# First chunk of a gated long convolution: q's rows in 128-partition transfers, let go by steps of step two

## The chip, the cores and the metric

The kernel runs on one core of one Trainium2 chip. The metric is the device time of one launch in microseconds (us): the median of three runs before the change is 697.23 us. Times inside the run come from one profiled execution and are counted from the start of its span. PE is the matrix engine (TensorE), DVE is VectorE, ACT is ScalarE, POOL is GpSimd, SP is SyncE, which here only starts transfers.

## The reference

What is computed, cut to what matters (B = 1, S = 2048 rows, D = 640 channels, F = 1728):

```python
x = A_q
mod = (_silu(c) @ w_mod).reshape(c.shape[0], 6, 1, -1)
sa, ca, ga, sb, cb, gb = (mod[:, i] for i in range(6))
h = _layernorm(x, axis=-1) * (1 + ca) + sa
# _A_ref: a 4-tap causal filter of k, times v, a long causal
# convolution with ssm_k per channel (by FFT), plus kv * ssm_D, times h
x = x + ga * _A_ref(h, A_k, A_v, A_shift_k, A_ssm_k, A_ssm_D)
h = _layernorm(x, axis=-1) * (1 + cb) + sb
# _B_ref: layernorm, then w2 @ gelu(w1 @ .) over the 2048 rows
x = x + gb * _B_ref(h, B_w1, B_b1, B_w2, B_b2)
```

So the first gate needs three things: q's rows with their mean and variance, the first half of `silu(c) @ w_mod` (1920 of its 3840 columns), and the long convolution.

## The kernel before, in words

**Tiling.** The 640 channels go in five chunks `c` of 128. A partition holds 64 positions of two half chunks of 64 channels; q's 2048 rows lie in two tiles `xa` and `xb` (views `XH`, `XR(j)`) with row `32*i + 16*b + j` in partition `64*b + i`, column block `j` (0 to 15).

**One chunk of the convolution.** `kv_ops` multiplies k's four taps and v into `X` (four groups of 8 operations; group 2 often on POOL, the others on DVE, in part handed out between other work by `dv(n)` from the list `fill`). `step1(0, t)` transforms `X` on PE (line 230), `step1(1, t)` the filter `ssm_k`, which `load_ks` brings into `aux`, `perm_add` adds `ssm_D` to, and `perm` lays into the tile `p`. Step two is `f2(g)`, g = 0 to 7 (line 246): 64 matmuls into PSUM, one half copied out by ACT (`kt`), two products by DVE (`p`), two additions by POOL (`y`). `i2` (line 275) and `i1` (line 294) transform back, and `gate` multiplies into `A1` (the second half of `aux`) and adds to x.

**The first chunk has more in it.** While chunk 0 goes through step two, q is loaded. Its statistics (`bn_stats`, 16 column blocks, two reads and one merge each) come on DVE behind the loop, `rstd` after them. `mod_load` brings w_mod's 1920 columns in five pieces of 128 rows (983,040 bytes each), `mod_part` multiplies each on PE (line 354) as soon as its turn in PE's order comes, `mod_sum` and `mod_row` (line 365) spread the sums to all partitions, then `a1_ops` makes the normalised rows (`ac`, on ACT, from `rs1` and `nm1`) and scales them (`po`, on DVE).

**What sets the order.** It is written out by hand: every engine runs its instructions in program order. SP's transfers share eight semaphores in turn, so a transfer is started only when the one eight places before it has landed, and a wait of one transfer holds all behind it. The constant of step two, `c_w2`, arrives in two halves of 1 MB in columns 1024 to 5119 of `xb`, is laid out by ACT (`lay_w2`), and then its place is taken by q's rows 9 to 15. `load_taps`, `load_ks`, `load_k`, `load_v` and `load_halo` (the only one with 63 rows) bring the rest.

The transfers that the change is about are these:

```python
def load_q():
    for j in range(16):
        for b in range(2):
            sync.dma_start(XH[j // 8][64 * b:64 * b + 64, j % 8], dram(q, (16 * b + j) * D, [[32 * D, 64], [1, D]]))
    for kk in range(4):
        mod_load(0, kk, (T_v1[:, 0:1920], T_v1[:, 1920:3840], T_aux[:, 0:1920], T_aux[:, 2048:3968])[kk])
```

Of the kernel before, what the change touches and what calls it, by code (L numbers as in the profile page):

```python
# [50 lines left out]
def mixer_kernel(ctx: ExitStack, tc: tile.TileContext, q, k, v, shift_k, ssm_k, ssm_D, w1, b1, w2, b2, c,  # L51
# [110 lines left out]
    def load_ks(c, eng=sync):  # L162
        for h in range(2):
            sync.dma_start(KSR[64 * h:64 * h + 64].rearrange("p (i n) -> p i n", i=64),  # L164
                           dram(ssm_k, (DC * c + 64 * h) * S, [[32, 64], [S, 64], [1, 32]]))
        for h in range(2):
            eng.dma_start(DR[64 * h:64 * h + 1], dram(ssm_D, DC * c + 64 * h, [[64, 1], [1, 64]]))
# [143 lines left out]
    def gate(c, ps, half, eng=pool, j0=0, j1=8, then=()):  # L311
# [3 lines left out]
        for f_ in then:  # L315
            f_()
        x = XH[half][:, j0:j1, DC * c:DC * c + DC]
        TT(eng, x, x, a, ALU.add)
# [15 lines left out]
    def rstd(r, nm, j0, n, between=()):  # L334
# [4 lines left out]
        pool.tensor_scalar(v_, v_, EPS, None, op0=ALU.add)  # L339
# [138 lines left out]
    run(kv_ops(3))  # L478
    kv_loads(1, 3)
    load_w2c(1)  # L480
# [4 lines left out]
    sync.dma_start(stg[30:35, :], dram(c, 0, [[128, 5], [1, 128]]))  # L485
# [12 lines left out]


    three = lambda t: [t[:, 640 * j:640 * j + 640] for j in range(3)]  # L500
    pl = [three(t) for t in (T_v1, T_v1[:, 1920:3840], T_aux, T_aux[:, 2048:3968], P)]

    def load_q():
        for j in range(16):
            for b in range(2):
                sync.dma_start(XH[j // 8][64 * b:64 * b + 64, j % 8], dram(q, (16 * b + j) * D, [[32 * D, 64], [1, D]]))
        for kk in range(4):
            mod_load(0, kk, (T_v1[:, 0:1920], T_v1[:, 1920:3840], T_aux[:, 0:1920], T_aux[:, 2048:3968])[kk])
# [3 lines left out]
    def dv(n):  # L512
        for _ in range(min(n, len(fill))):
            fill.pop(0)()

    x1s = lambda c, j: lambda: dve.bn_stats(bst[:, j, c, :], XR(j, DC * c, DC))
    for c in range(NC):
# [3 lines left out]
        for g in range(8):  # L521
# [27 lines left out]
        if c == 0:  # L549
            for j in range(16):  # L550
                for h in range(2):
                    dve.bn_stats(bst[:, j, h, :], XR(j, 320 * h, 320))
                dve.bn_aggr(mv[:, j, :], bst[:, j, 0:2, :])
# [4 lines left out]
        if c == 0:  # L558
            mod_load(0, 4, P[:, 0:1920])
            for t in range(4):  # L560
                step1(0, t)
            ps = psum()
# [610 lines left out]
```

## Time and profile before

| what | value |
|---|---|
| median of three runs | 697.23 us (696.96 to 703.46) |
| the profiled execution's own time | 693.24 us |
| its span, first to last instruction | 691.5 us |
| PE busy | 634.1 us, 92% of the span |
| DVE, ACT, POOL busy | 510.9, 312.4, 155.3 us |
| chunk 0: step one begins, step two begins | 23.60, 41.65 us |
| chunk 1: step two begins | 106.72 us |
| moved by transfers | 95.91 MB in 173,552 packets |

The profiled execution is 4 us shorter than the median of the runs. A row of the timeline gives the start of a group of instructions, the time from its start to its end, the engine, the line, the operation, out<-in with the shapes and the count; in brackets stands the idle time before it and what ended it. A group of PE counts each matmul of this kernel's first part twice, as two passes. A row of the windows gives for one stretch the busy time of each engine, the granted PE clock (1.00 is full), the mean busy share of the 16 transfer engines (it can be a little over 1) and what they moved in GB/s.

### The profile page before, as it was taken

The page shows a single profiled execution, that of the slowest core. Times are in us where ns is not written, and L with a number is a line of the kernel's source. Part 1 is how long each engine was busy: PE and PEld are TensorE (multiplying, and loading weights), DVE is VectorE, ACT ScalarE, POOL GpSimd, SP SyncE. Part 2 cuts the span into 40 slices and gives each one's busy share as a digit, 9 for nine tenths or more (in the row PEclk, how much of TensorE's full clock was granted, in tenths as well). Part 3 has the DMA queues.
Part 4 walks back from the last instruction along what each step waited for, and adds up shares of the span by engine and source line. Part 5 has one row for each costly group of instructions (what it writes and reads, how often), then busy time and mean ns, then how long its engine had stood idle before and what let it go on. Part 6 is the DMA issues. An engine that isn't in the chain of part 4 may idle for free.

```text
span 691.5 us, 20713 instructions
## 1 busy us (share of the span) xinstructions
PE 634.1 (92%) x9057; PEld 614.7 (89%) x9057; DVE 510.9 (74%) x857; ACT 312.4 (45%) x467; POOL 155.3 (22%) x137
## 2 busy tenths in 40 slices
PE   0699979889999999987999999999999999999997
PEld 0699679789999999776899999999999999999997
DVE  6678669869879837888896430676489888888886
ACT  0664575545645635554776520543334333333331
POOL 5298039615625526300000000000000000000000
PEclk9999889999999999999999999999999999999999
DMA  9978988637242523353021832378679653455511
GB/s 181 207 218 237 345 161 163 140 63 161 51 78 81 173 49 94 117 116 69 5 58 35 149 69 55 76 210 188 204 258 362 190 160 107 126 166 174 169 43 39
DMA packets 173552, 95.91 MB, mean 139 GB/s; under 512 B 89715, under 2 KB 163222, under 8 KB 173462
## 3 DMA queue, kind: packets, MB, share of 16 engines
q1 hardware_dynamic: 168914, 93.28, 52.0%
q10 hardware_dynamic: 4548, 1.31, 1.1%
q8 instruction: 71, 1.16, 0.7%
q14 instruction: 19, 0.16, 0.1%
HBM read 77.53 MB, written 17.04 MB: 137 GB/s over the span
## 4 chain that ended last, share of the span: by engine, by line
PE 67%; DVE 14%; POOL 8%; ACT 4%; issue 3%; SPq 2%; DMA 1%; ACTq 0%; DVEq 0%; POOLq 0%
PE pst L1074 25%; PE pst L437 18%; PE pst L230 7%; POOL y L60 6%; PE pst L246 5%; PE pst L275 5%; PE pst L939 3%; DVE tap L60 3%; PE pst L294 2%; DVE kt L60 2%; POOL t L60 1%; SPq L164 1%; DMA in<-in_A_k_dram 1%; PE tap L354 1%; DVE y L60 1%
## 5 line engine op out<-in xcount | busy, mean ns | idle before, releaser
L246 PEld LDWEIGHTS pst<-z,w 128*64 128x64 f32 x2560 | 94.7, 141 | 8.4 <-ACT z L232 7.3
L246 PE MATMUL pst<-z,w 128*64 128x64 f32 x2560 | 95.7, 240 | 6.9 <-ACT z L232 6.1
L60 POOL TENSOR_TENSOR y<-p 128x256 f32<-128x256 f32 x72 | 91.3, 1307 | 22.3 <-DVE p L60 21.9
L60 DVE TENSOR_TENSOR p<-pst,kt 128x512 f32<-128x512 f32 x80 | 53.0, 690 | 22.6 <-ACT kt L250 14.5
L230 PE MATMUL pst<-v,x 128*64 128x128 f32 x640 | 45.1, 300 | 23.8 <-DVE x L60 23.6
L230 PEld LDWEIGHTS pst<-v,x 128*64 128x64 f32 x640 | 43.3, 222 | 24.3 <-POOL t L462 23.6
L232 ACT ACTIVATE z<-pst 128x1024 f32<-128x1024 f32 x40 | 45.8, 1144 | 40.1 <-PE pst L230 20.4
L250 ACT ACTIVATE kt<-pst 128x512 f32<-128x512 f32 x40 | 25.1, 628 | 46.4 <-PE pst L246 21.2
L275 PEld LDWEIGHTS pst<-v,y 32*128 32x128 f32 x1280 | 39.6, 193 | 7.1 <-POOL y L60 4.3
L275 PE MATMUL pst<-v,y 32*128 32x64 f32 x1280 | 41.6, 279 | 4.1 <-DVE y L60 3.2
L230 PE MATMUL pst<-v,p 128*64 128x128 f32 x640 | 37.3, 274 | 2.9 <-issue 1.7
L230 PEld LDWEIGHTS pst<-v,p 128*64 128x64 f32 x640 | 35.0, 137 | 3.9 <-issue 2.2
L1074 PE MATMUL pst<-r_z,m_w 128*128 128x320 f32 x198 | 37.2, 309 | 0.0
L60 DVE TENSOR_TENSOR tap<-tap,kt 128x512 f32<-128x512 f32 x51 | 35.5, 697 | 1.3
L60 DVE TENSOR_TENSOR kt<-in,tap 128x512 f32<-128x512 f32 x51 | 35.0, 687 | 1.5
L283 ACT ACTIVATE z<-pst 128x512 f32<-128x512 f32 x38 | 21.3, 659 | 24.5 <-PE pst L275 24.5
L1074 PEld LDWEIGHTS pst<-r_z,m_w 128*128 128x128 f32 x198 | 31.1, 188 | 0.0
L1011 ACT ACTIVATE m_w<-m_v 128x896 fp32r<-128x896 f32 x19 | 17.9, 948 | 23.6 <-DVE m_v L60 13.1
L294 PEld LDWEIGHTS pst<-z,v 64*64 64x64 f32 x1280 | 22.4, 145 | 6.2 <-issue 3.2
L294 PE MATMUL pst<-z,v 64*64 64x64 f32 x1280 | 24.2, 231 | 2.8 <-issue 1.7
L437 PE MATMUL pst<-r_z,wb 128*128 128x320 f32 x144 | 23.3, 319 | 2.6 <-DVE aux L60 1.7
L60 DVE TENSOR_TENSOR m_w<-m_v,m_w 128x896 fp32r<-128x896 f32 x19 | 20.6, 1087 | 6.5 <-ACT m_w L1011 6.5
(300 smaller groups left out, 1429.1 us busy)
## 6 DMA issues: line engine op xcount, KB each, us to landing
x<-in_B_w_dram SPq DMA_DIRECT2D x20, 512.0 KB
m_v<-in_B_w_dram SPq DMA_DIRECT2D x20, 384.0 KB
aux<-in_A_ssm_k_dram SPq DMA_DIRECT2D x10, 512.0 KB
out_dram<-m_w SPq DMA_DIRECT2D x32, 160.0 KB
in<-in_A_k_dram SPq DMA_DIRECT2D x36, 128.0 KB
in<-in_A_v_dram SPq DMA_DIRECT2D x36, 128.0 KB
ts<-m_p SPq DMA_DIRECT2D x10, 320.0 KB
m_w<-xs SPq DMA_DIRECT2D x20, 160.0 KB
```

The lines of the kernel that those rows point to most:

```text
L60: TT = lambda eng, o, a, b, op: eng.tensor_tensor(o, a, b, op=op)
L230: pe.matmul(ps[64 * ri:64 * ri + 64, o:o + 128], lhs, F1[:, 128 * ri:128 * ri + 128], start=True, stop=True)
L232: evac = lambda: act.activation(Z[:, side, t].rearrange("p a k e -> p e a k"), ps.rearrange("p (e a k) -> p e a k", a=8, e=2), AF.Copy)
L246: pe.matmul(ps[64 * h:64 * h + 64, o:o + 64], W2[k1 // 32][:, 2 * (k1 % 32) + ri], rhs, start=True, stop=True)
L250: act.activation(kt.rearrange("p (m i) -> p m i", i=32), pv[:, :, 1], AF.Copy)
L275: pe.matmul(pp[qd // 2][:, o:o + 64], Y[p, ri, i:i + 2].rearrange("p i k -> p (i k)"), V2[p, 64 * ri:64 * ri + 64], start=ri == 0, stop=ri ...
L283: act.activation(o, i, AF.Copy)
L294: pe.matmul(ps[64 * b:64 * b + 64, 512 * e + 64 * jj:512 * e + 64 * jj + 64], V1[p, ri, n2], T2[p, :, 32 * ri + n2], start=ri == 0, stop=r ...
L437: pe.matmul(ps[0:m, h, 0:320], w_.bitcast(F32R), r_[:, 320 * h:320 * h + 320].bitcast(F32R), start=first and i == 0, stop=last and i == 2)
L939: pe.matmul(ps[n][:, h, 0:320], sets[n][:, j].bitcast(F32R), r[:, 320 * h:320 * h + 320].bitcast(F32R), start=j == 0 and r is hh, stop=j = ...
L1011: act.activation(W[n][0].bitcast(F32R), A[p, w_], AF.Copy)
L1074: pe.matmul(bank[n], w[:, i].bitcast(F32R), r.bitcast(F32R), start=m == 0 and k == 0, stop=m == 6 and k == 2)
```

## The change

q's 16 column blocks are loaded by one transfer each instead of two: both blocks of 64 rows, 128 partitions, with the source written as 2 blocks of 64 rows of 640 numbers. The first eight follow the small constants at once. The other eight go in pairs, and w_mod's first three pieces between them, each released by a small write of ACT (`paced`) in steps 0 to 6 of step two. The second half of `c_w2` goes ahead of the last group of k and v loads. w_mod's pieces get other places, so that `aux`'s first half is free for `load_ks`. `load_taps(2)` moves behind q's first half. The transpose and the `silu` of c go into step two, three of the statistics too; POOL's filter group 2 for chunk 2 comes ahead of `perm_add`; two of `mod_part` come ahead of `i2(0)`; `rstd`'s addition and half of `i2(1)`'s copies go to DVE, and so do chunk 0's additions to x, behind both gates.

```diff
     def load_ks(c, eng=sync):
         for h in range(2):
+            eng.dma_start(DR[64 * h:64 * h + 1], dram(ssm_D, DC * c + 64 * h, [[64, 1], [1, 64]]))
+        for h in range(2):
             sync.dma_start(KSR[64 * h:64 * h + 64].rearrange("p (i n) -> p i n", i=64),
                            dram(ssm_k, (DC * c + 64 * h) * S, [[32, 64], [S, 64], [1, 32]]))
-        for h in range(2):
-            eng.dma_start(DR[64 * h:64 * h + 1], dram(ssm_D, DC * c + 64 * h, [[64, 1], [1, 64]]))
...
+    def add_x(c, half, eng=dve, j0=0, j1=8):
         x = XH[half][:, j0:j1, DC * c:DC * c + DC]
-        TT(eng, x, x, a, ALU.add)
+        TT(eng, x, x, A1[:, 8 * half + j0:8 * half + j1], ALU.add)
...
-        pool.tensor_scalar(v_, v_, EPS, None, op0=ALU.add)
+        eng.tensor_scalar(v_, v_, EPS, None, op0=ALU.add)
...
     run(kv_ops(3))
+    load_w2c(1)
     kv_loads(1, 3)
-    load_w2c(1)
...
+    def load_q(j0, j1):
+        for j in range(j0, j1):
+            sync.dma_start(XH[j // 8][:, j % 8], dram(q, j * D, [[16 * D, 2], [32 * D, 64], [1, D]]))
+
+    load_q(0, 8)
     perm_add(0)
     perm(0)
     all_taps()
-    load_taps(2)
     for t in range(4):
         step1(0, t)
         lay_w2(0, t)
+    load_taps(2)
...
+    wm = (T_v1[:, 0:1920], T_v1[:, 1920:3840], T_aux[:, 2048:3968], P[:, 0:1920])
+    pl = [three(t) for t in wm] + [[T_in[:, 1728:2368], T_in[:, 2368:3008], T_kt[:, 640:1280]]]
+
+    def paced(g):
+
+        if g in (2, 4, 6):
+            act.activation(wm[g // 2 - 1][:, 0:1], epsc, AF.Copy)
+            mod_load(0, g // 2 - 1, wm[g // 2 - 1])
+        elif g in (0, 1, 3, 5):
+            j = (8, 10, 0, 12, 0, 14)[g]
+            act.activation(XR(j, 0, 1), epsc, AF.Copy)
+            load_q(j, j + 2)
...
             if c == 0 and g < 4:
                 lay_w2(1, g)
-                if g == 3:
-                    load_q()
+            if c == 0:
+                paced(g)
+            if c == 0 and g == 1:
+                ps = psum()
+                pe.transpose(ps[:, 0:36], stg, ID[0:36, 0:36])
+                act.activation(cols, ps[:, 0:36], AF.Copy)
+                act.activation(sil, cols[:, 30:35], AF.Silu)
             dv(-(-len(fill) // max(6 - g, 1)))
+            if c == 0 and g > 4:
+                q_stats(g - 5)
...
         if c == 0:
+            load_k(2, 1)
+            load_k(2, 2)
+            load_v(2, 2)
+            mod_load(0, 3, wm[3])
+            for j in range(3):
+                sync.dma_start(pl[4][j], dram(w_mod, 512 * 6 * D + 640 * j, [[6 * D, 128], [1, 640]]))
+            for j in range(3, 16):
+                q_stats(j)
...
             for t in range(4):
                 step1(0, t)
+            pool.tensor_scalar(PW, TR.rearrange("p (i s) -> p s i", s=4), 1.0, None, op0=ALU.mult)
+            run(kv_ops(2, pool))
+            mod_part(tap, 0, pl[0])
+            mod_part(tap, 1, pl[1])
+            sync.dma_start(T_v1[:, 0:4096], c_v1, max_dma_last_dim=4096)
+            load_ks(1)
             i2(0)
+            mod_part(tap, 2, pl[2])
+            rstd(rs1, nm1, 0, 16, eng=dve)
+            run(ac[0:2])
+            i2(1, dve)
+            mod_part(tap, 3, pl[3])
             mod_part(tap, 4, pl[4])
...
+            run(ac[2:8])
             mod_sum(tap, T_kt[:, 0:640])
...
-            run(po)
+            run(po[0:2])
...
-            gate(c, ps, half)
+            elif half:
+                run(po[2:4])
+            gate(c, ps, half, pool if c else None)
+        if c == 0:
+            add_x(c, 0)
+            add_x(c, 1)
```

In SP's order, from the last of the small constants (`in_c`) to the filter of chunk 1, before:

```order
L485 DMA g<-in_c_dram 5x128
L160 DMA rows<-in_A_shift_k_dram 64x256 x2
L506 DMA xa<-in_A_q_dram 64x640 x16
L506 DMA xb<-in_A_q_dram 64x640 x16
L347 DMA v<-in_w_mod_dram 128x3x640 x2
L347 DMA aux<-in_w_mod_dram 128x3x640 x2
L347 DMA p<-in_w_mod_dram 128x3x640
L570 DMA v<-in_const_v_dram 128x4x1024
L164 DMA aux<-in_A_ssm_k_dram 64x64x32 x2
```

The same stretch after the change:

```order
L489 DMA g<-in_c_dram 5x128
L493 DMA xa<-in_A_q_dram 128x1x640 x8
L160 DMA rows<-in_A_shift_k_dram 64x256 x2
L493 DMA xb<-in_A_q_dram 128x1x640 x4
L351 DMA v<-in_w_mod_dram 128x3x640
L493 DMA xb<-in_A_q_dram 128x1x640 x2
L351 DMA v<-in_w_mod_dram 128x3x640
L493 DMA xb<-in_A_q_dram 128x1x640 x2
L351 DMA aux<-in_w_mod_dram 128x3x640
L144 DMA in<-in_A_k_dram 64x8x64 x4
L150 DMA in<-in_A_v_dram 64x8x64 x2
L351 DMA p<-in_w_mod_dram 128x3x640
```

Sixteen transfers of q stand for 32, the taps of chunk 2 (`shift_k`) behind eight of them, w_mod's first piece behind twelve, its third behind all sixteen, and six loads of k and v for chunk 2 ahead of its fourth.

PE's order where chunk 1's step one (line 230, from `x`) ends, before:

```order
L230 MATMUL pst_794<-v,x 64x128 x16
L230 MATMUL pst_812<-v,x 64x128 x16
L563 MATMUL pst_830<-v,g 128x36
L275 MATMUL pst_834<-v,y 128x64 x2
L275 MATMUL pst_835<-v,y 128x64 x2
```

And after, where line 358 is `mod_part` with pieces 0 and 1 of w_mod:

```order
L230 MATMUL pst_797<-v,x 64x128 x16
L230 MATMUL pst_815<-v,x 64x128 x16
L358 MATMUL tap<-v,sm 32x320 x12
L275 MATMUL pst_859<-v,y 128x64 x2
L275 MATMUL pst_860<-v,y 128x64 x2
```

The transpose of the small constants (line 563) has left this place for step two, and `i2(0)` (line 275) now stands behind two of w_mod's pieces.

More of the change, by code (lines that the diff above doesn't have):

```diff
@@ L514, in dv, with q_stats @@
             fill.pop(0)()
+    def q_stats(j):
+        for h in range(2):
+            dve.bn_stats(bst[:, j, h, :], XR(j, 320 * h, 320))
+        dve.bn_aggr(mv[:, j, :], bst[:, j, 0:2, :])
     x1s = lambda c, j: lambda: dve.bn_stats(bst[:, j, c, :], XR(j, DC * c, DC))
```

35 lines of the change are left out of this document (3 added, 32 removed).

## The prediction

> **What bounds the kernel now.** I read the page's chain first, then PE's timeline between chunk 0's step two and chunk 2's, then the other engines and the transfers in the same stretch.
>
> ```profile
> PE 67%; DVE 14%; POOL 8%; ACT 4%; issue 3%; SPq 2%; DMA 1%; ACTq 0%; DVEq 0%; POOLq 0%
> 60.52 8.34 PE L230 MATMUL pst<-v,x 128*64 128x128 f32 x128
> 70.03 5.41 PE L275 MATMUL pst<-v,y 32*128 32x64 f32 x124 [0.62 <-ACT z L232]
> 75.38 3.99 PE L354 MATMUL tap<-v,sm 128*32 128x320 f32 x24
> 79.20 2.32 PE L354 MATMUL tap<-aux,sm 128*32 128x320 f32 x24
> 81.45 3.80 PE L275 MATMUL pst<-v,y 32*128 32x64 f32 x128
> 85.18 1.28 PE L354 MATMUL tap<-p,sm 128*32 128x320 f32 x12
> 88.08 1.71 PE L365 MATMUL pst<-kt,sm 1*128 1x320 f32 x12 [1.62 <-ACT kt L358]
> 90.52 6.57 PE L294 MATMUL pst<-z,v 64*64 64x64 f32 x256 [0.73 <-ACT g L372]
> 98.33 7.21 PE L230 MATMUL pst<-v,p 128*64 128x128 f32 x128 [1.23 <-ACT p L176]
> 106.72 14.39 PE L246 MATMUL pst<-z,w 128*64 128x64 f32 x384 [1.19 <-ACT z L232]
> 133.34 4.09 PE L275 MATMUL pst<-v,y 32*128 32x64 f32 x128 [1.75 <-DVE y L60]
> 160.81 19.01 PE L246 MATMUL pst<-z,w 128*64 128x64 f32 x511 [1.24 <-ACT z L232]
> 185.01 3.58 PE L275 MATMUL pst<-v,y 32*128 32x64 f32 x120 [0.71 <-DVE y L60]
> ```
>
> Two thirds of the chain are PE's. Between 60.52 and 106.72 PE waits four times for 0.6 to 1.6 us and then 1.2 for step two: some 5.4 us is all that better ordering could take out here. No wait is for q or for w_mod: both come in time. Chunk 1's stretch from step two to `i2` is 133.34 - 106.72 = 26.6 us, chunk 2's 185.01 - 160.81 = 24.2: another 2.4 us. These are the gains on offer. The margin on the other side is how early q and w_mod arrive:
>
> ```profile
> 36.89 0.31 SPq L485 DMA_DIRECT2D g<-in_c_dram  x1
> 37.51 3.21 SPq L160 DMA_DIRECT2D rows<-in_A_shift_k_dram  x2
> 40.77 11.62 SPq L506 DMA_DIRECT2D xa<-in_A_q_dram  x16
> 52.43 11.79 SPq L506 DMA_DIRECT2D xb<-in_A_q_dram  x16
> 64.27 1.12 SPq L347 DMA_DIRECT2D v<-in_w_mod_dram  x2
> 62.77 0.88 DVE L552 BATCH_NORM_STATS2 sm<-xa 128x6 f32<-128x320 f32 x2
> 78.69 0.21 DVE L553 BATCH_NORM_AGGREGATE sm<-sm 128x2 f32<-128x12 f32 x1
> ```
>
> SP starts q's 32 halves between 40.77 and 64.22, 0.73 us apart. w_mod follows at 64.27, and its first piece is used at 75.38: eleven microseconds from the start of the transfer to its use. The statistics (last row) end at 78.9, just before `i2(1)`.
>
> **The transfers of q.** The last rows that I need are those on how a transfer is spread over the 16 engines:
>
> ```profile
> 44.00:57.00 13.00, 13.00 (x361) 13.00 (x357) 10.24 (x17) 8.38 (x10) 12.92 (x10) 1.00 0.84 230
> 70.00:71.00 1.00, 0.97 (x36) 0.97 (x36) 0.97 (x4) 0.98 (x2) 0.00 (x0) 1.00 1.02 407
> DMA packets 423, 0.11 MB, mean 87 GB/s; under 512 B 379, under 2 KB 423, under 8 KB 423
> 163.00:163.80 0.80, 0.80 (x29) 0.80 (x25) 0.77 (x2) 0.34 (x1) 0.00 (x0) 1.00 0.39 86
> 164.60:165.00 0.40, 0.40 (x17) 0.40 (x14) 0.40 (x2) 0.24 (x1) 0.00 (x0) 1.00 1.11 252
> ```
>
> While q's 64-row halves run (44 to 57) a share of 0.84 of all engines is busy; w_mod's 128-row pieces (70 to 71) fill them. The packet row is the stretch 162.8 to 164.1, whose 379 short packets are chunk 4's two halos, 2 x 63 rows x 3 pieces = 378. While these alone run (163.0 to 163.8) the share is 0.39; when the 64-row loads of k follow (164.6), with packets of the same 256 bytes, it is 1.11. A transfer of 63 rows does not get sixteen engines. The largest number up to 16 that divides 63 is 9, and 9/16 = 0.56 bounds 0.39. So the outermost dimension seems to be dealt out in equal whole parts. The source of the new q transfer has 2 as its outermost dimension (two blocks of 64 rows), the old one 64. Two equal parts are two engines; that is what I forecast. Every transfer of the kernel before has the same outermost count on both sides, so no row shows what a 2 on one side and 128 on the other do; that is the open point, and its other answer is the first rival.
>
> [...]
>
> **Its price.** A transfer is 128 x 2560 = 327,680 bytes, 163,840 for each of two engines. For one engine's speed there are two rows: 407 GB/s over 16 full engines is 25.4 GB/s; 230 over 16 x 0.84 is 17.1. Both move packets of 2560 bytes. I take 25.4, since w_mod's rows too are queued many deep on each engine, as q's would be: 163,840 / 25.4 = 6.45 us, and sixteen 103.2. Each w_mod piece queued between them puts 61,440 bytes on each engine, 2.42 us, three 7.3. SP was done with the small constants at 37.20; the wait of `load_taps` there was for `c_w2`, which is ahead now, so I let q begin at 39. Eight transfers may be under way, so the two engines never run dry, and the third piece lands at 39 + 103.2 + 7.3 = 149.5. PE stands before piece 0 until 39 + 12 x 6.45 + 2.4 = 119, and before piece 1 until 134; `i2(0)`, behind them, falls in between.
>
> From 149.5 on, on the same two engines: six loads of k and v of 8,192 bytes per engine at 252/16 = 15.8 GB/s, 0.52 each, 3.1; pieces 3 and 4, 4.8. So `mod_part(4)` ends near 158.7 against 85.18 + 1.28 = 86.46 before: 72.2 later. The constant `v1` (2 MB, 5.2 us) lands at 162.7, where `i1` began at 90.52: 72.2 too. The filter of chunk 1 queues behind it:
>
> ```profile
> 96.10 2.17 ACT L176 ACTIVATE p<-aux 128x2048 f32<-128x2048 f32 x1 [1.97 <-POOL aux L60]
> 106.51 5.08 SPq L164 DMA_DIRECT2D aux<-in_A_ssm_k_dram  x2
> ```
>
> With 6 us for its two transfers (5.08 to start them, and landing), 1 for `perm_add` and 2.2 for `perm`, `step1(1)` starts at 172 against 98.33. The latest of the three decides: 73 to 74, I take 73.
>
> **The other parts** ride under that wait:
>
> ```profile
> 35.20 2.52 POOL L60 TENSOR_TENSOR t<-in,t 128x512 f32<-128x512 f32 x2 [11.83 <-DMA in<-in_A_k_dram]
> 45.99 20.52 POOL L60 TENSOR_TENSOR y<-p 128x256 f32<-128x256 f32 x16
> 109.79 2.51 POOL L60 TENSOR_TENSOR xa<-xa,aux 128x1024 f32<-128x1024 f32 x1
> 112.26 2.48 POOL L60 TENSOR_TENSOR xb<-xb,aux 128x1024 f32<-128x1024 f32 x1
> 92.09 5.06 DVE L60 TENSOR_TENSOR aux<-aux,g 128x1024 f32<-128x1024 f32 x4
> 37.50:39.50 2.00, 2.00 (x41) 2.00 (x38) 1.93 (x3) 1.39 (x2) 1.84 (x3) 1.00 0.98 392
> 69.87 0.19 ACT L564 ACTIVATE sm<-pst 128x36 f32<-128x36 f32 x1
> 70.08 1.28 ACT L565 ACT_TABLE_LOAD   x1
> 89.96 2.61 SPq L167 DMA_DIRECT2D rows<-in_A_ssm_D_dram  x2
> ```
>
> - `c_w2`'s second half ahead: 1 MB at 392 GB/s, 2.7 us, in front of the k that POOL waits for at 35.20. POOL's additions then end at 69.2, not 66.5; step two loses 0 to 1 us. Hidden as long as PE waits for w_mod.
> - The taps of chunk 2 land behind eight q transfers, at about 39 + 51.6 = 91; POOL's whole queue (the taps' copy, filter group 2, `perm_add(1)`) stands behind them, then behind k and v at 152.6, and needs 1.1 + 8 x 1.3 = 11.5: free at 164, before the filter lands. Nothing.
> - Seven ACT writes of one column: under 0.19 each, in idle time. Transpose, table load and `silu`, 1.7 us of ACT, between two copies of step two: 0 to 0.5.
> - Statistics: 16 x 1.0 us; the last waits for q's last transfer, landing at 147, before piece 2. Three of them stand in front of products of step two; q's third lands at 58, and that product ran at 61.49: nothing.
> - `ssm_D` ahead of the filter takes 2.6 us out of SP's way to it; it is in the order used above.
> - The additions to x: 4.99 us off POOL, 2 x 1.27 onto DVE (5.06 / 4). POOL's backlog was what held chunk 1: 0 to 2.4 us won; DVE's own list is longer by 2.5 and half of `i2`'s copies, so I take 2.
>
> Sum against the profiled execution: 693.24 + 73 - 2 = 764. The runs' median lies 4 us above that execution, so 768.
>
> **Rivals.**
>
> 1. *Sixteen engines after all* (the side that is not slower). If transfers are dealt out by the partitions of the tile, q and three pieces of w_mod, 8.2 MB at 392 GB/s, 21 us, are in by 63, and q binds nothing. Then `mod_part` and `i2` run without a gap to 83.6, the statistics end at 79, and the rows of `mod` are spread some 2.5 us earlier than at 88.08; DVE's list behind them ends as before, so step two of chunk 1 gains 2.5, and POOL's missing backlog 2: 693.24 - 4.5 = 689, 693 as a median. For it: w_mod's 128-row rows fill all engines. Against: the halos. It decides from the point where q needs less than 35 us. Chance 0.08.
> 2. *Sixteen engines, but the gain is given back*: POOL late by 2.7 us holds the last products of step two, and the clock that fell to half in this stretch falls again:
>
> ```profile
> 72.00:76.00 4.00, 4.00 (x70) 3.54 (x69) 3.86 (x13) 0.91 (x2) 0.00 (x0) 0.50 1.05 400
> ```
>
>    `i2` took 5.41 us there, mostly at that clock, and 3.80 right after. Then 689 + 2.7 + 1.6 = 693, 697 as a median. Chance 0.04.
> 3. *Two engines at the slower speed.* With 17.1 GB/s a transfer takes 9.58 us; sixteen and three pieces take 164.1 instead of 110.5, and what follows 5 more: 764 + 58 = 822, 826 as a median. For it: it is q's own row. Against: there SP started a transfer only every 0.73 us, with four packets an engine. Chance 0.12.
>
> **How the numbers follow.** Two engines near 25 GB/s have 0.76, rival 3 0.12, rivals 1 and 2 together 0.12. The fast end of the two-engine case is the highest value within 66 to 71, 451 GB/s or 28.2 an engine: 768 - 12 = 756. With a little on either side the range is 752 to 828; it leaves out the first two rivals and a twentieth beyond its ends. About 1% (7 us) is what a measurement of this kernel can tell from no change. Faster by more than that needs more than rival 1's sum: 0.03; within 1%: 0.09; slower: 0.88.
>
> ```profile
> DMA  3769549988999999999989998999999999999999
> GB/s 102 123 205 246 164 184 328 287 307 287 369 369 389 369 430 389 389 410 430 389 328 389 451 369 328 451 451 369 348 451 451 369 410 430 410 389 451 410 389 369
> ```
>
> **What would show it.** Right: from about 45 to 150 us the busy share of the engines stays near 2/16 = 0.13 and the rate near 50 GB/s; PE's first `mod_part` waits for `v<-in_w_mod_dram` for some 50 us; SP's q transfers come 6.5 us apart; chunk 1's step two begins near 180. Rival 3 shows the same at 34 GB/s, rival 1 q's last statistics before 80 and shares near 1. The prediction is wrong in its root if q's transfers reach more than two engines, and in its size if the rate on two engines is not 51 GB/s.

## The result, and the profile after

The changed kernel takes 778.83 us (median of four runs, 774.74 to 779.49), the kernel before 697.10 on the same chip (four runs). The ratio, taken over the fast runs alone (one of the kernel before, 703.46 us, counts as slow and is left out), is 1.119 with a 95% interval of 1.115 to 1.124. The forecast was 768 within 752 to 828: direction and mechanism as written there, 11 us too low. The profiled execution took 779.34 us, its span is 777.5 against 691.5: 86.0 us more.

The page's shares of the chain, for the kernel after (before: PE 67%, SPq 2%):

```profile
PE 54%; SPq 16%; DVE 13%; DMA 6%; POOL 5%; ACT 3%; issue 2%; ACTq 0%; DVEq 0%; POOLq 0%
```

SP's queue, which had 2% of the chain, now has 16%, a hundred microseconds and more of a span of 777.5. The windows of the kernel after, in the stretch in which q is loaded, show how many engines carry it (the last three columns are the clock granted to PE, the mean busy share of the 16 transfer engines, and GB/s):

```profile
45.00:50.00 5.00, 5.00 (x133) 4.86 (x131) 4.42 (x7) 4.41 (x8) 4.84 (x5) 1.00 0.14 54
95.00:100.00 5.00, 0.00 (x0) 0.00 (x0) 1.10 (x3) 0.00 (x0) 1.09 (x1) 0.50 0.13 50
```

A share of 0.13 at 50 GB/s is two engines of sixteen at 25 GB/s each; before, the share in this place was 0.84. The second row also shows PE without work and its clock at half. DVE's timeline gives the time of one transfer, since each pair of `bn_stats` waits for the next transfer:

```profile
75.27 0.89 DVE L532 BATCH_NORM_STATS2 sm<-xa 128x6 f32<-128x320 f32 x2 [5.43 <-DMA xa<-in_A_q_dram]
95.12 0.89 DVE L532 BATCH_NORM_STATS2 sm<-xa 128x6 f32<-128x320 f32 x2 [5.43 <-DMA xa<-in_A_q_dram]
...
122.43 0.89 DVE L532 BATCH_NORM_STATS2 sm<-xb 128x6 f32<-128x320 f32 x2 [5.19 <-DMA xb<-in_A_q_dram]
132.67 0.89 DVE L532 BATCH_NORM_STATS2 sm<-xb 128x6 f32<-128x320 f32 x2 [9.10 <-DMA xb<-in_A_q_dram]
...
156.20 0.89 DVE L532 BATCH_NORM_STATS2 sm<-xb 128x6 f32<-128x320 f32 x2 [6.12 <-DMA xb<-in_A_q_dram]
```

From 75.27 to 95.12 lie three transfers, 6.62 us each: 163,840 bytes for each of two engines, so 24.7 GB/s. Between 122.43 and 132.67 a piece of w_mod went by as well: 10.24 - 6.62 = 3.6 us for it. The last statistics start at 156.20; before, they ended at 78.9.

PE's timeline and then the pieces of the chain in order of time (start, us, what), both of the kernel after:

```profile
124.98 2.35 PE L358 MATMUL tap<-v,sm 128*32 128x320 f32 x12 [55.61 <-DMA v<-in_w_mod_dram]
141.81 2.35 PE L358 MATMUL tap<-v,sm 128*32 128x320 f32 x12 [14.48 <-DMA v<-in_w_mod_dram]
...
159.13 2.36 PE L358 MATMUL tap<-aux,sm 128*32 128x320 f32 x12 [7.93 <-DMA aux<-in_w_mod_dram]
161.42 7.11 PE L275 MATMUL pst<-v,y 32*128 32x64 f32 x128
...
184.32 8.87 PE L230 MATMUL pst<-v,p 128*64 128x128 f32 x128 [3.00 <-ACT p L176]
194.38 14.38 PE L246 MATMUL pst<-z,w 128*64 128x64 f32 x384 [1.19 <-ACT z L232]
...
244.17 19.00 PE L246 MATMUL pst<-z,w 128*64 128x64 f32 x511 [1.24 <-ACT z L232]
...
268.36 4.62 PE L275 MATMUL pst<-v,y 32*128 32x64 f32 x120 [0.72 <-DVE y L60]
272.91 3.69 PE L230 MATMUL pst<-v,x 128*64 128x128 f32 x32
```

```profile
159.71 5.66 DMA p<-in_w_mod_dram
165.39 13.05 DMA aux<-in_A_ssm_k_dram
178.44 2.58 issue
181.01 1.17 POOL aux L60
182.21 2.07 ACT p L176
184.32 8.90 PE pst L230 x128
```

PE stands before the three pieces for 55.6, 14.5 and 7.9 us, 78 in sum. Behind the third piece come k and v for chunk 2, the fourth piece and the rest, the constant `v1`, the filter `ssm_k`, POOL's `perm_add`, ACT's `perm`, PE's step one. Step two of chunk 1 begins at 194.38 against 106.72: 87.7 us later, a little more than the whole loss. From there to chunk 2's step two it is 49.8 us against 54.1 before, 4.3 won; two rows of chunk 2 at half clock (4.62 and 3.69, against 3.58 and 2.26 before) give 2.5 back.

### The profile page after: what moved, and what is told of

It is laid out like the page before. It is cut to its first block, busy times and chain, and to the rows that moved or that the text cites. A ratio compares the mean times of both kernels' runs of the same rounds, so it can differ in the third digit from the quotient of the medians.

```text
span 777.5 us, 20692 instructions
## 1 busy us (share of the span) xinstructions
PE 647.5 (83%) x9057; PEld 625.2 (80%) x9057; DVE 515.4 (66%) x862; ACT 311.8 (40%) x472; POOL 151.2 (19%) x134
## 4 chain that ended last, share of the span: by engine, by line
PE 54%; SPq 16%; DVE 13%; DMA 6%; POOL 5%; ACT 3%; issue 2%; ACTq 0%; DVEq 0%; POOLq 0%
PE pst L1101 21%; PE pst L441 17%; SPq L493 10%; POOL y L60 4%; PE pst L230 4%; PE pst L275 4%; PE pst L966 3%; PE pst L246 3%; SPq L351 3%; DMA in<-in_A_k_dram 2%; DVE tap L60 2%; PE pst L294 2%; DMA aux<-in_A_ssm_k_dram 2%; DVE kt L60 2%; SPq L144 2%
## 5 line engine op out<-in xcount | busy, mean ns | idle before, releaser
L230 PE MATMUL pst<-v,x 128*64 128x128 f32 x640 | 46.4, 306 | 23.6 <-DVE x L60 23.6
L230 PEld LDWEIGHTS pst<-v,x 128*64 128x64 f32 x640 | 44.4, 220 | 24.1 <-POOL t L466 23.6
L358 PE MATMUL tap<-v,sm 128*32 128x320 f32 x24 | 4.7, 739 | 70.1 <-DMA v<-in_w_mod_dram 70.1
L275 PEld LDWEIGHTS pst<-v,y 32*128 32x128 f32 x1280 | 45.6, 221 | 6.7 <-issue 3.5
L275 PE MATMUL pst<-v,y 32*128 32x64 f32 x1280 | 47.5, 308 | 2.2 <-DVE y L60 2.1
L532 DVE BATCH_NORM_STATS2 sm<-xb 128x6 f32<-128x320 f32 x16 | 7.1, 486 | 52.0 <-DMA xb<-in_A_q_dram 52.0
L60 POOL TENSOR_TENSOR t<-in,t 128x512 f32<-128x512 f32 x12 | 15.2, 1280 | 82.2 <-DMA in<-in_A_k_dram 67.0
```

What stands on the lines that cost most here:

```text
L60: TT = lambda eng, o, a, b, op: eng.tensor_tensor(o, a, b, op=op)
L230: pe.matmul(ps[64 * ri:64 * ri + 64, o:o + 128], lhs, F1[:, 128 * ri:128 * ri + 128], start=True, stop=True)
L275: pe.matmul(pp[qd // 2][:, o:o + 64], Y[p, ri, i:i + 2].rearrange("p i k -> p (i k)"), V2[p, 64 * ri:64 * ri + 64], start=ri == 0, stop=ri ...
```

## The experiments

Every run was compared with the kernel before on the same chip; the chips differ from row to row, so rows are compared by their ratios. "Step two of chunk 1" is abbreviated as f2(1) in the table; its start is that of the profiled execution.

| run | what | median us | ratio [95% interval] | f2(1) at |
|---|---|---|---|---|
| before | | 697.1 | 1 | 106.72 |
| after | | 778.83 | 1.119 [1.115, 1.124] | 194.38 |
| e1_two_alone | before + q's new form alone | 779.27 | 1.119 [1.111, 1.127] | 189.61 |
| e2_halves | after, q in the old 32 halves | 693.55 | 0.996 [0.992, 1.000] | 107.32 |
| e3_sixteen | after, q in 16 transfers, 64 outermost | 699.97 | 1.005 [1.001, 1.009] | 118.74 |
| e4_dose | after, first half of q on 8 and 4 engines | 719.53 (one run) | | 135.80 |
| e5_dve_adds | before + additions to x on DVE | 691.72 | 0.993 [0.989, 0.996] | 104.42 |
| e6_pool_adds | e2 with the additions on POOL | 694.93 | 0.999 [0.995, 1.002] | 111.53 |
| e7_pairs | after, q in 16 transfers of 64 x 5,120 bytes | 700.26 | 1.007 [1.003, 1.010] | 115.88 |
| e8_reordered | e2, loads and sums reordered | 690.30 | 0.990 [0.985, 0.994] | 104.52 |
| e9_keep_clock | after + 528 idle matmuls | 802.42 | 1.153 [1.147, 1.160] | 216.20 |
| e10_half_dose | after, only q's first half in the new form | 738.37 | 1.061 [1.057, 1.065] | 154.61 |
| e11_two_queues | e7, half of it started by ACT | 705.56 | 1.013 [1.009, 1.017] | 120.70 |
| e12_keep_clock_sized | after + 360 idle matmuls | 776.50 | 1.118 [1.113, 1.124] | 192.12 |

**Is it the form of q's transfers, and that alone?** First the kernel before with q's new form and nothing else:

```diff
-            for b in range(2):
-                sync.dma_start(XH[j // 8][64 * b:64 * b + 64, j % 8], dram(q, (16 * b + j) * D, [[32 * D, 64], [1, D]]))
+            sync.dma_start(XH[j // 8][:, j % 8], dram(q, j * D, [[16 * D, 2], [32 * D, 64], [1, D]]))
```

> The kernel before with nothing changed but q's transfers: 16 of 128 partitions, the source as 2 blocks of 64 rows. Theory A (the outermost count 2 leaves two engines to a transfer): q starts at 41, sixteen transfers of 6.6 us end at 147, w_mod's first four pieces queue behind all of them at 3.4 us each and end near 160; the first matrix product with w_mod waits to about 150; 775 to 800 us. Rival B (q's form is harmless, the waits in the changed kernel come from the released order of q, w_mod and the taps): no slower than before, 690 to 700 us.

It took 779.27 us, the changed kernel's time. PE's timeline of this run:

```profile
154.88 3.85 PE L354 MATMUL tap<-v,sm 128*32 128x320 f32 x24 [80.23 <-DMA v<-in_w_mod_dram]
```

Here all of w_mod stands behind q, so PE has one long wait, of 80.2 us. Then the other way round: the changed kernel with `load_q` back in halves.

```diff
-            sync.dma_start(XH[j // 8][:, j % 8], dram(q, j * D, [[16 * D, 2], [32 * D, 64], [1, D]]))
+            for b in range(2):
+                sync.dma_start(XH[j // 8][64 * b:64 * b + 64, j % 8], dram(q, (16 * b + j) * D, [[32 * D, 64], [1, D]]))
```

> The changed kernel with q's transfers alone put back to 32 of 64 rows; all other edits stay. Theory A: q fills over 0.8 of all engines and is in by about 65; no wait for w_mod; 685 to 695 us, which is what all the other edits are worth together. Rival B: the order and the releases stay, so the waits stay: above 750 us.

It took 693.55 us, 0.996 of before. In its PE timeline the first products with w_mod follow step one without a wait, and step two of chunk 1 begins at 107.32:

```profile
69.20 2.35 PE L358 MATMUL tap<-v,sm 128*32 128x320 f32 x24
...
107.32 14.38 PE L246 MATMUL pst<-z,w 128*64 128x64 f32 x384 [1.18 <-ACT z L232]
```

The two runs together settle the cause: the form by itself makes the whole loss, and without it the rest of the change loses nothing and may gain 2 to 3 us. The bytes and rows are the same in sum; what differs is 2 or 64 as the outermost count of the source, and with it the number of transfers (16 or 32), their size and the partitions that each writes (128 or 64). Number and size are ruled out by e3 below, with 16 transfers of the same size and 64 outermost (699.97 us); w_mod's pieces, which write 128 partitions, run at a share of 1.02.

**Does the price follow the number of such transfers?** Two doses. The first loads q's first half in blocks of 8 and of 4 partitions, with 20,480 bytes in each row:

```diff
+        if j1 - j0 == 8:
+            for b, n in ((0, 8), (1, 4)):
+                for i in range(0, 64, n):
+                    sync.dma_start(T_x[0][64 * b + i:64 * b + i + n, :],
+                                   dram(q, (32 * i + 16 * b) * D, [[32 * D, n], [1, 8 * D]]))
+            return
...
```

The other half comes as 64 rows by two column blocks, 64 outermost.

> The changed kernel with tile xa loaded in 8-partition transfers (first half, 8 of 163,840 bytes) and 4-partition transfers (second half, 16 of 81,920 bytes), all contiguous rows of 20 KB; xb as 64 rows by two blocks. Theory A: the busy share is near 8/16 = 0.50 and the rate near 200 GB/s for some 7 us, then 0.25 and 100 GB/s for some 13 us; nothing waits long, 690 to 710 us. Rival C: contiguous patterns of two dimensions run at full share, 0.8 or more, whatever their outermost count.

Windows of this run, in the part with 8 and the part with 4 partitions:

```profile
54.00:57.00 3.00, 3.00 (x89) 3.00 (x85) 2.21 (x4) 0.93 (x4) 3.00 (x4) 1.00 0.54 74
60.00:63.00 3.00, 0.51 (x15) 0.36 (x10) 0.00 (x0) 0.00 (x0) 1.54 (x2) 1.00 0.22 41
...
66.00:69.00 3.00, 0.00 (x0) 0.00 (x0) 0.00 (x0) 0.00 (x0) 0.00 (x0) 0.50 0.24 89
```

The shares fit 8/16 and 4/16 (0.42 to 0.63 in the windows from 42 to 57, 0.22 to 0.26 from 60 to 72), so the equal whole parts of the prediction fit at three counts (2, 4 and 8). The rate does not follow: 74 GB/s on eight engines is 9 GB/s each, where two engines gave 24.7 each. As a measure of the price the run is a miss (690 to 710 us were expected); as a finding it comes up again below. The second dose keeps the new form for q's first half and loads the other in halves:

```diff
-        for j in range(j0, j1):
-            sync.dma_start(XH[j // 8][:, j % 8], dram(q, j * D, [[16 * D, 2], [32 * D, 64], [1, D]]))
+        for j in range(j0, min(j1, 8)):
+            sync.dma_start(XH[0][:, j], dram(q, j * D, [[16 * D, 2], [32 * D, 64], [1, D]]))
+        for j in range(max(j0, 8), j1):
+            for b in range(2):
+                sync.dma_start(XH[1][64 * b:64 * b + 64, j - 8], dram(q, (16 * b + j) * D, [[32 * D, 64], [1, D]]))
```

> The changed kernel with q's first eight column blocks as it has them (2 blocks of 64 rows in the source) and the other eight as 16 halves of 64 rows. Theory (each such transfer costs 6.6 us on two engines, the rest of q and w_mod little): the first eight take from 40 to 93, the sixteen halves and three pieces about 14 more on the two busy engines, so the third piece lands near 107 instead of 159; chunk 1's step two begins at 140 to 146, and the time is 722 to 732 us. Rival (the halves queue behind in a way that costs as much as the whole, or the first eight ride under step two for nothing): above 745 or below 705 us.

```profile
106.89 2.36 PE L358 MATMUL tap<-v,sm 128*32 128x320 f32 x12 [37.92 <-DMA v<-in_w_mod_dram]
112.77 2.35 PE L358 MATMUL tap<-v,sm 128*32 128x320 f32 x12 [3.52 <-DMA v<-in_w_mod_dram]
115.05 7.11 PE L275 MATMUL pst<-v,y 32*128 32x64 f32 x128
```

At 738.37 us it lies 6 above the theory's range and below the rival's. From no such transfers to eight the time rises by 738.37 - 693.55 = 44.8 us, from eight to sixteen by 40.5; eight transfers of 6.62 us are 53. So the price grows with their number, by somewhat less than they take. What the theory had too short is the rest of q and w_mod: it let the third piece land near 107, but PE still waits for the second until 112.77. From 100 to 115 us the engines run at a share of 1.00 to 1.07 and move 288 to 300 GB/s, not the 407 of w_mod's pieces in the kernel before. From the second piece on PE waits for no transfer, but runs both `i2` and the products of w_mod at half clock.

**What does the half clock cost?** In the changed kernel `i2(1)` takes 7.11 us where it took 3.80. The next kernels add matmuls of constants that nobody reads, ahead of the pieces of w_mod, so that PE stays busy while it waits:

```diff
+    def keep(n):
+        for _ in range(n):
+            ps = psum()
+            for i in range(8):
+                pe.matmul(ps[0:64, 128 * i:128 * i + 128], F1[:, 64:128], F1[:, 0:128], start=True, stop=True)
...
+            keep(46)
             mod_part(tap, 0, pl[0])
+            keep(11)
             mod_part(tap, 1, pl[1])
...
+            keep(9)
             mod_part(tap, 2, pl[2])
```

> The changed kernel with 528 extra matmuls on PE that nobody reads (constants times constants, 0.13 us each by the rows of step one), 48 us of them ahead of the first w_mod piece's products, 11.5 ahead of the second's, 9.4 ahead of the third's, so that PE is busy while it waits for q and w_mod. In the changed kernel the granted clock is 0.50 from 73 to 172 us and i2(1) takes 7.11 us there against 3.80. Both theories: the clock stays at 1.00 and i2(1) takes 3.8. Theory A (the half clock is in the path: i2(1), two pieces' products and step one): 5 to 7 us are won, chunk 1's step two begins at 188 to 190 instead of 194.4, 773 us. Rival B (the filter's transfers are last there, ACT lays them out at 182.2, and only step one's 1.7 us can be won): step two begins at 192 to 193.5, 776 to 778 us.

```profile
68.44 80.40 PE L513 MATMUL pst<-v 128*64 128x128 f32 x735
148.77 1.28 PE L358 MATMUL tap<-v,sm 128*32 128x320 f32 x12
```

The clock stayed up (0.987 as a mean, 0.915 without them), but 735 of the profile's records, two to a matmul, took 80.40 us: 0.218 us a matmul, not the 0.13 that I had sized them by. They ran 24 us past the landing of the first piece, and the run is 23.6 us longer than the changed kernel. (Step one's matmuls write to both halves of PSUM's partitions in turn, these to one; whether that is the difference was not tried.) With 31, 7 and 7 in place of 46, 11 and 9:

> The run with extra matmuls again, fewer of them: in it one took 0.218 us, not 0.13, so that they ran on until 148.8 where the first piece had landed by 125, and the pieces came late by them. Now 248, 56 and 56 of them: 54, 12 and 12 us, which end at about 123, 138 and 159, when the three pieces land. All theories: the clock stays near 1.00 and i2(1) takes 3.8 us against 7.11. Theory A (the half clock is in the path): chunk 1's step two begins at 188 to 190 instead of 194.4, 772 to 775 us. Rival B (the filter's transfers and its layout on ACT, done at 184.3 in the changed kernel, are last): only step one's 1.7 us are won, step two begins at 192 to 193.5, 776 to 778 us. Rival C (the extra matmuls cost what they save, by their own loads or by a wait): 778 us or above.

```profile
160.53 3.80 PE L275 MATMUL pst<-v,y 32*128 32x64 f32 x128
...
183.73 7.21 PE L230 MATMUL pst<-v,p 128*64 128x128 f32 x128 [3.31 <-ACT p L176]
192.12 14.37 PE L246 MATMUL pst<-z,w 128*64 128x64 f32 x384 [1.18 <-ACT z L232]
```

`i2(1)` is back at 3.80, but step one still begins at 183.73 (184.32 in the changed kernel), since it waits for `p`, that is for the filter. Only step one's own 8.87 - 7.21 = 1.7 us come out, and step two begins at 192.12, as rival B had it. In the changed kernel, then, the half clock takes about 2 us (the medians, 776.50 and 778.83, do not tell the two apart); the queue of transfers up to the filter sets the rest. In the half dose PE does not wait for `p`, but there too the filter is close behind; POOL's last addition to it and ACT's `perm` in e10:

```profile
139.04 0.43 POOL L60 TENSOR_TENSOR aux<-aux,rows 1x64 f32<-1x64 f32 x1 [2.42 <-issue]
142.46 2.19 ACT L176 ACTIVATE p<-aux 128x2048 f32<-128x2048 f32 x1
```

ACT begins `p` 3.0 us after the filter is ready, and step one follows it at 144.90. By these rows, as an estimate, the half clock cost at most about 3 us before step one there as well.

**What are the other edits worth?** The kernel before with the additions to x on DVE alone:

```diff
-            gate(c, ps, half)
+            gate(c, ps, half, pool if c else dve)
```

> The kernel before with one edit: chunk 0's two additions to x go to DVE, each right behind its gate. Theory A (POOL's backlog is what holds chunk 1; the additions are the part of the change that is worth something): chunk 1's stretch from the start of step two to i2 falls from 26.6 us to 24 to 25, the rest stays, ratio 0.996 to 0.998. Rival B (the gain of the variant with halves comes from the reordering of i2, mod_part and the filter, not from the additions): the stretch stays within 0.5 us of 26.6, because DVE is then as late as POOL was, ratio 0.999 to 1.002. In both, step two of chunk 1 begins within 1 us of 106.7.

```profile
104.42 12.01 PE L246 MATMUL pst<-z,w 128*64 128x64 f32 x320 [1.19 <-ACT z L232]
...
129.13 0.45 PE L275 MATMUL pst<-v,y 32*128 32x64 f32 x8
```

The stretch from step two to `i2` is 24.7 us against 26.6, as theory A had it. POOL begins with the sums of chunk 1 at 109.4 and not at 114.7. In sum the run is faster than A allowed, 0.993 with an interval that ends at 0.996: step two also begins 2.3 us earlier, since the half clock in `i2(0)` and in the products behind it (5.41 and 3.99 us before) didn't come in the profiled execution (3.79 and 2.35). Whether that belongs to the edit or to chance was not tried; the runs of the kernel before beside it lie between 691.84 us at a mean clock of 0.992 and 700.08 at 0.968, so chance is not ruled out. The complement, e2 with the additions on POOL again:

```diff
-            gate(c, ps, half, pool if c else None)
-        if c == 0:
-            add_x(c, 0)
-            add_x(c, 1)
+            gate(c, ps, half)
```

> The changed kernel with q in 64-row halves (as in the run that came to 0.9964) and with chunk 0's two additions back on POOL, each behind its gate. Theory A: the additions were all of its gain, so ratio 0.999 to 1.002 and chunk 1's stretch from step two to i2 is again 26 to 27 us, against 24.1 in the run with the additions on DVE. Rival B: the gain stays, ratio 0.995 to 0.998.

```profile
94.63 6.03 PE L294 MATMUL pst<-z,v 64*64 64x64 f32 x256 [3.49 <-DMA v<-in_const_v_dram]
...
111.53 14.38 PE L246 MATMUL pst<-z,w 128*64 128x64 f32 x384 [1.18 <-ACT z L232]
...
135.41 4.16 PE L275 MATMUL pst<-v,y 32*128 32x64 f32 x128
```

The time (0.999) fits theory A, but its mechanism does not: the stretch stays at 23.9 us with the additions on POOL, most likely because there filter group 2 is out of POOL's way by then. Step two itself begins later than in e2, behind waits for w_mod and the constant `v1`. The two medians differ by 1.4 us with overlapping intervals, so what the additions are worth on top of the reordering isn't settled; taking them off POOL (e5) or making the other edits, POOL's group 2 earlier among them (e6), each shortens that stretch by about 2 to 3 us, and e2, with both, is no shorter (24.1).

**A better version.** e2 with chunk 2's first three loads behind the pieces of w_mod again, POOL's group 2 behind `perm_add`, and the sums of `mod` ahead of six normalisations on ACT:

```diff
-            load_k(2, 1)
-            load_k(2, 2)
-            load_v(2, 2)
             mod_load(0, 3, wm[3])
...
-            run(kv_ops(2, pool))
             mod_part(tap, 0, pl[0])
...
             mod_part(tap, 4, pl[4])
+            mod_sum(tap, T_kt[:, 0:640])
+            load_k(2, 1)
+            load_k(2, 2)
+            load_v(2, 2)
             load_halo(2)
...
             run(ac[2:8])
-            mod_sum(tap, T_kt[:, 0:640])
             perm_add(1)
+            run(kv_ops(2, pool))
```

> The changed kernel with q in halves and two reorderings: the three loads of k and v for chunk 2 and POOL's filter group 2 go back behind the last w_mod piece and perm_add, as in the kernel before, and the sums of mod are made on ACT ahead of six normalisations. In the run with halves PE waited 2.47 us for those sums, 1.54 for the constant v1, and 2.29 for the filter. Theory (these waits are in the path): 3 to 5 us are won, step two of chunk 1 begins at 103 to 105 instead of 107.3, ratio 0.990 to 0.993. Rival (POOL's group 2, now behind perm_add, comes late for chunk 1 and gives it back): step two begins early but chunk 1 takes 2 to 4 us longer, ratio 0.995 to 0.999.

```profile
85.54 1.43 PE L369 MATMUL pst<-kt,sm 1*128 1x320 f32 x12 [0.90 <-ACT kt L362]
88.44 3.52 PE L294 MATMUL pst<-z,v 64*64 64x64 f32 x142 [1.46 <-ACT g L376]
```

690.30 us, 0.990 of before (0.985 to 0.994), the lowest median of the study; its interval overlaps that of e5 (0.989 to 0.996), so it is not shown to beat that one edit. In its PE timeline the wait for the sums is 0.90 (2.47 in e2), the one for `v1` gone, and step two begins at 104.52, as the theory had it. From there to `i2` it is 25.2 us against 24.1 in e2, so a part of what the rival expected, POOL's group 2 coming late, is given back.

**Fewer transfers, but spread over sixteen engines.** Two forms with 64 as the outermost count and twice the bytes in each transfer. In e3, shown here, a transfer of the first half brings two column blocks four apart (in the second half, neighbours); in e7 it is always two neighbours, 5,120 bytes in one piece:

```diff
-        for j in range(j0, j1):
+        s = 4 if j1 - j0 == 8 else 1
+        for j in range(j0, j0 + (j1 - j0) // 2):
             for b in range(2):
-                sync.dma_start(XH[j // 8][64 * b:64 * b + 64, j % 8], dram(q, (16 * b + j) * D, [[32 * D, 64], [1, D]]))
+                sync.dma_start(XH[j // 8][64 * b:64 * b + 64, j % 8:j % 8 + s + 1:s],
+                               dram(q, (16 * b + j) * D, [[32 * D, 64], [s * D, 2], [1, D]]))
```

> The changed kernel with the same number of q transfers (16), the same bytes in each (327,680) and, for tile xa, the same packets of 2560 bytes in a pattern of three dimensions, but with 64 outermost (64 rows, two column blocks) instead of 2. Theory A: like the 32 halves, 685 to 695 us. Rival C (a pattern of three dimensions that cannot be merged is what is slow, or the size of a transfer): xa's transfers stay near 50 GB/s and the time stays above 730 us.

> The changed kernel with q in 16 transfers of 64 rows and two neighbouring column blocks, whose source rows are 5,120 bytes in one piece: the same bytes per transfer as in the run with 16 transfers of 64 rows and two apart blocks (699.97 us, PE without a released wait for 13 us in step two), 64 as the outermost count on both sides. Theory (those gaps of PE came from the slow two-piece pattern of q's first half, 220 GB/s at a share of 1.06): q's first half goes at 350 GB/s or more, PE's unexplained gaps between 40 and 112 us are under 2 us, ratio 0.993 to 0.999 as with the halves. Rival (they came from the bytes under way, 2.6 MB of q at once rather than 1.3): gaps of 8 us or more again, ratio 1.002 to 1.008.

Both lose against the 32 halves: 699.97 and 700.26 us. But both lie far below the 730 us of e3's rival C: neither the number of transfers nor their size nor a pattern that can't be merged is what made the changed kernel slow. Here the windows from 44 to 57 us, of e7 and then of e2:

```profile
44.00:57.00 13.00, 10.98 (x291) 10.70 (x288) 8.19 (x13) 8.89 (x16) 12.68 (x10) 1.00 1.01 247
```

```profile
44.00:57.00 13.00, 13.00 (x352) 12.86 (x348) 9.58 (x16) 9.98 (x18) 12.84 (x10) 1.00 0.76 210
```

and PE's timeline of e7:

```profile
52.79 4.94 PE L246 MATMUL pst<-z,w 128*64 128x64 f32 x128 [2.02 <-issue]
60.71 4.86 PE L246 MATMUL pst<-z,w 128*64 128x64 f32 x127 [2.98 <-issue]
69.80 2.29 PE L246 MATMUL pst<-z,w 128*64 128x64 f32 x37 [4.23 <-issue]
```

The engines are busy without a break, yet move only 247 GB/s against 210 in e2, and PE stands for 9.2 us in step two with no wait that the profile shows (12.0 up to 112 us); e2 has 0.3 up to there. Since e7 has no two-piece pattern, the theory that the pattern makes the gaps falls; the rival, the bytes under way, fits both runs. How they could hold PE, the transfers of instructions suggest. The profile's row for these in e7, from 50.0 to 52.8 us:

```profile
q8 instruction: 1, 0.02, 2.8%
```

Each of the three stops has one such load of 16,384 bytes. By their packets in the trace they end at 51.42, 59.24 and 68.49, and PE goes on 1.3 to 1.5 us after each; e3's stops end the same way. In e2 three such loads lie between 44 and 57 us and PE does not stop. So PE seems to stand for instructions that come late; no edit tested it.

The last run of this kind had half of e7's transfers started by ACT:

```diff
-                sync.dma_start(XH[j // 8][64 * b:64 * b + 64, j % 8:j % 8 + 2],
+                (sync, act)[b].dma_start(XH[j // 8][64 * b:64 * b + 64, j % 8:j % 8 + 2],
```

> The run with pairs (q in 16 transfers of 64 rows by 5,120 bytes, 700.26 us, 240 to 280 GB/s at a full share, PE without a released wait for 10.5 us) with one edit: the eight transfers into partitions 64 to 127 are started by ACT, so that both halves of the partitions are written at the same time. Theory P (what is slow is the side of the partitions that is written: 64 partitions take only half of what 128 do, so both sides at once run faster): while q is loaded the rate is 330 to 420 GB/s at the same share, and PE's unexplained gaps in step two fall under 4 us; 692 to 697 us. Rival R (the source rows are slow to read, or the bytes under way are what matters): still 240 to 290 GB/s and gaps of 8 us or more; 699 us or above.

```profile
55.27 0.29 PE L565 MATMUL pst<-v,g 36*128 36x36 f32 x1 [6.39 <-DMA g<-in_B_b_dram]
```

It does not tell the theories apart. ACT's first four stand so early in its order that they went ahead of k and the small constants, for which PE then waited 6.39 us; the second half came one or two at a time between w_mod's pieces, so no stretch shows q written to both sides alone at a full share. The gaps (1.97 and 2.64 us in step two, 0.78 behind it) lie between the two expectations.

## Why the prediction came out as it did

**Two engines: right, and shown.** The share is 0.13 to 0.14, 2/16, e1 and e2 isolate the form, and e4's shares continue the row to 4 and 8. The semaphore events of the traces agree: after its start, each of q's sixteen transfers adds two increments as it lands, e4's of four and eight rows four and eight, a halo of 63 rows nine, and a load of 64 rows or a piece of w_mod sixteen. The equal whole parts that the prediction took from the halos fit these runs at 2, 4, 8 and 64 as the outermost count. One transfer of 128 partitions for two on disjoint halves, which the first rival held to be no slower, costs 12% with this source (e1).

**The speed of an engine: near.** 24.7 GB/s against 25.4 taken; the third rival's 17.1 is out.

**The landing of the third piece: the term that was mis-sized.** "The third piece lands at 39 + 103.2 + 7.3 = 149.5" was the step; PE takes it at 159.13, 9.6 us later. Sixteen transfers at 6.62 instead of 6.45 make 2.7 of that. The pieces took about 3.6, 3.3 and 2.9 us (10.24 and 9.95 between statistics, less 6.62; 159.13 - 156.20), 9.8 against 7.3: 2.5. The start makes 3.2: counted back from the fourth landing, 68.70 - 4 x 6.62 = 42.2, since the first transfer's way to landing comes on top of 39. Some 1 us remains, 0.3 of it the taps of chunk 2 behind the eighth transfer (102.03 - 95.12 = 6.91).

**From there to the filter: 2.7 us short; behind it right, but for the clock.** Between the third piece and the filter's landing the prediction had 162.7 + 6 - 149.5 = 19.2 us. The chain ends the load at 178.44, 19.3 after the piece, but that is where POOL's first addition ends. POOL then stands for 2.58 us, and the chain names no releaser for that. The windows of the changed kernel show what was still under way:

```profile
171.50:174.50 3.00, 2.10 (x21) 1.06 (x15) 0.00 (x0) 1.19 (x3) 0.07 (x1) 0.97 1.32 205
174.50:177.00 2.50, 1.80 (x63) 1.58 (x64) 1.57 (x3) 2.34 (x5) 0.00 (x0) 0.62 0.24 38
177.00:179.50 2.50, 2.26 (x102) 2.13 (x99) 2.46 (x2) 2.04 (x6) 1.05 (x1) 0.70 1.28 203
```

The filter comes in two halves of 524,288 bytes, and 203 GB/s over 2.5 us is about one of them: the second half arrives only after 177, and POOL's second addition needs it. In e8 the same stop is put down to that load:

```profile
91.16 0.36 POOL L60 TENSOR_TENSOR aux<-aux,rows 1x64 f32<-1x64 f32 x1 [2.16 <-DMA aux<-in_A_ssm_k_dram]
```

So the filter is complete when that addition starts, at 181.01, 21.9 us after the third piece and not 19.2. The term to look at is the 6 us for its two transfers, which went by 5.08 us for starting chunk 2's. Chunk 1's own took 9.40 to start in the kernel before, and 12.45 after the change:

```profile
80.50 9.40 SPq L164 DMA_DIRECT2D aux<-in_A_ssm_k_dram  x2
163.43 12.45 SPq L166 DMA_DIRECT2D aux<-in_A_ssm_k_dram  x2
```

Why the second half starts late was not tried. From 181.01 to step one it is 3.3 us, as the 3.2 for `perm_add` and `perm` had it. The half clock in step one, 1.7 us, was not in the sum; e12, 2.3 us earlier at step two, shows that little more than that is on the path, though `i2(1)` lost 3.3.

Together: 9.6 + 2.7 + 1.7 and 0.7 from taking 73 for 73.7 make 14.7 us, and step two of chunk 1 began at 194.4, not at 179.7.

**POOL's backlog: right in sign, 4.3 and not 2, and not by the additions alone.** From step two of chunk 1 to that of chunk 2 it is 54.1 us before, 52.1 with the additions on DVE alone (e5), 50.0 with all other edits and the additions still on POOL (e6), 50.1 with both (e2) and 49.8 in the changed kernel. So the additions are worth 2 by themselves, as taken, but the rest of the change gives the whole gain without them. Filter group 2, which the prediction put at nothing and which is earlier on POOL here, fits that; it was not moved alone. That 2 had the right sign is in part luck. The half clock in chunk 2 (2.5) was not foreseen. 764 + 14.7 - 2.3 + 2.5 = 778.9 against 779.3 measured.

**The first rival's price: right as a number, by luck.** With sixteen engines the prediction had 689 for a profiled execution and 693 as a median; the halves give 690.31 and 693.55. Its way there was another, though: step two did not begin 2.5 us earlier, since PE waited 2.47 us for the sums, 1.54 for `v1` and 2.29 for the filter, and chunk 1's stretch was 2.5 shorter instead. These waits are what e8 took up.

## What to carry to other kernels

Before two transfers are joined into one, look at the outermost count of the source, not at the number of partitions alone: with 2 there, q's transfers into 128 partitions held the engines at a share of 0.13, with 4 and 8 (e4) at 0.22 to 0.26 and 0.42 to 0.63, with 64 at 0.76 (e2) to 1.01 (e7), and such a flat share in the windows gives it away at once. When a late transfer is moved in a queue, sum the whole queue behind it up to the last consumer; here that sum was 2.7 us short of 21.9, and its head landed 9.6 us late, 3.2 of it because the way to the first landing was left out. Take each term from a row of the same transfer: the filter's went by another chunk's. And a wait of PE can cost twice, once as a wait and once as half clock in the work behind it (`i2(1)` 7.11 us against 3.80), though here the filter's transfer was later still: with the clock kept up (e12) step two began only 2.3 us earlier.

## What the runs showed of the hardware beyond that

- The speed of an engine is not one number. Two engines moved 24.7 GB/s each in the changed kernel; in e4 the 8-row transfers moved 74 GB/s at a share of 0.54, 9 for each of eight engines, and the 4-row ones first 41 and later 89 at 0.22 and 0.24, 10 and 22 for each of four, in one and the same form. Loads into 64 partitions moved 247 GB/s at a share of 1.01 (e7) and 210 at 0.76 (e2); the 128-partition pieces of w_mod moved 407 at 1.02. Whether the side of the partitions that is written makes that difference, e11's theory P, no run shows: 247 is 0.61 of 407, not half, and e11, which was meant to tell the side from the form and the bytes of the transfers, did not bring both sides under load. Nor is it known why e4's four engines got faster.
- With 327,680 bytes in each of q's transfers and the engines at a share of 1.0, PE stopped three times in step two for 2.0 to 4.2 us without a released wait (e3, e7), each time until 1.3 to 1.5 us after a load of instructions had ended. That its instructions arrive late behind the queued transfers fits these rows, but no run tested it.
- After the wait of 55.6 us the clock stayed at half for two bursts of work: `i2(0)` and `i2(1)` both took 7.11 us, and the last w_mod products were back at full clock (0.44 us a pair of records) only near 172, some 13 us after the third piece had landed. In e1, after 80.2 us, the first two pieces' 24 records took 3.85 us and the next piece's 12 were at 1.28, so there it was back within about 4. Why it took three times as long in the one case is open.
